# Chunks of one step in a message-passing kernel, and products of constants ahead of two groups of matmuls

## The chip, the cores and the metric

The kernel runs on one core of one Trainium2 chip. The metric is the device time of one execution in microseconds. Before the change the median of three runs is 8919.56 us (8911.16 to 8920.2).

## What is computed

One layer of message passing over a graph of 12500 nodes and 800000 edges, with 64 values per node and 16 per edge. `src` and `dst` are drawn at random, so a node has some 64 edges that come in, in no order.

```python
def reference(x, e_attr, src, dst, w_msg, w_upd):
    N, D = x.shape
    m_in = jnp.concatenate([x[src], x[dst], e_attr], axis=-1)
    msg = _silu(m_in @ w_msg)
    agg = _segment_sum(msg, dst, N)
    return _silu(jnp.concatenate([x, agg], axis=-1) @ w_upd)
```

## The kernel before, in words

**Tiles and buckets.** The edges stand in 6250 tiles of 128. The nodes are split into 128 buckets of 98 nodes (`BK`). Two flows run through one another. The first sorts the edges by the bucket of `dst` into a store in DRAM (`st`). The second reads sorted tiles of the store, works out their messages, and adds them by node into `ACC` on the chip.

**The sort, in steps of 8 tiles (`M`).** A step passes through three calls of `period`: first `onehot` (ACT, L396 and L397) makes `hf`, the one-hot matrix of buckets, and `sums` (L399) adds up to three of its tiles in bfloat16 into `G`. One period later `count` (L418, PE) multiplies these by a triangle and by ones (`onesb`) into `z`, so that `ranks` (L433, DVE) reads the rank of each edge within its bucket and chunk, and `expand` (L435 to L447, DVE) writes the edge's record of 17 numbers (`R`) into the slot of that rank in `X`, which has two buffers. Another period later `move` (L463, PE) multiplies `hf` and `X` into `pl`, in float32: row b of `pl` then holds the records of bucket b. When a chunk ends, ACT copies `pl` to `blk` (L468, two buffers), `place` (L481 and L482, DVE) moves the pointers of the buckets on, and in the next period POOL writes `blk` to the store by one indirect DMA (L486, the scatter).

**Chunks.** The slots of a chunk are shared by its tiles. The first 140 chunks (`N8`) are one step of 8 tiles, with 24 slots at their end. The rest are 12 tiles (`C`), a step and a half, with 30 slots at the end; the limit grows along the chunk (`LIM`: 13, 17, 21, 24, 27, 30, each for two tiles), and the product of a tile is 2 + 17 times its limit columns wide, 223 to 512. A step of this part stands in one of three places against the chunks (`turn` 0, 1, 2). Where a chunk goes on from the step before, the last sum of that step is carried over (`before`, L414, and L409 and L410 through the buffer `Gs`), and `count` adds it by a product of its own (L428). In `turn` 1 a chunk ends in the middle of the step, and `move` is called twice, around the product of the other flow.

**The batches.** A batch is 8 tiles of the store (6 in the second of three stages). POOL gathers a row of 64 values per edge by eight indirect DMAs (L649) into one of four buffers `g`, so the first of them waits for the sums by node of the batch four before. A period later PE transposes the batch's one-hot matrix and edge values (`tq`, L668), ACT copies them (`qt`, L671), and `product` (L677, PE) multiplies them with the weights into `pre`. Then `message` adds `pre` to `g` (L681, DVE) and applies silu (L682, ACT), and a period later `reduce` (L698, PE) sums by node into `ag`, which `add` (L710, DVE) adds to `ACC`.

**The order of the work.** `period` (L715) writes one call's instructions in a fixed order, and each engine takes its own in that order. On POOL that is four gathers, the scatter of a chunk that ended in the period before, four gathers. On PE it is `count`, the transposes, `reduce`, `move`, `product`. There are 782 steps, and 63 batches are left when the last is done. The lines on which the change turns are these:

```python
                for k in reversed(range(c.n)) if whole else range(c.n):
                    n = c.pos[k]
                    if part is not None and part != (c.turn == 1 and k >= C - M):
                        continue
                    ...
                    if ends:
                        w = 2 + LIM[c.size - 1] * R
                        end = Chunk(*c.last.values())
```

Of the kernel before, what the change touches and what calls it, by code (L numbers as in the profile page):

```python
# [3 lines left out]
F32 = mybir.dt.float32  # L4
# [19 lines left out]
C = 12  # L24
N8 = 140
LIM = [k for k in (13, 17, 21, 24, 27, 30) for _ in range(2)]
S = LIM[-1]
S8 = LIM[M - 1]
# [12 lines left out]
RK = float(C * P)  # L41
# [7 lines left out]
def mpnn_kernel(tc, x, e_attr, src, dst, w_msg, w_upd, out):  # L49
# [4 lines left out]
    assert E % P == 0 and NB <= NBK and NT >= C  # L54
    K8 = min(N8, NT // (2 * M))
    NCH = K8 + (NT - K8 * M + C - 1) // C
    CAPT = (K8 * S8 + (NCH - K8) * S) // P + 2
# [15 lines left out]
    with es:  # L73
# [43 lines left out]
        limc = cp.tile([P, 4, M], F32, name="limc")  # L117
        for k in range(4 * M):
            nc.vector.memset(limc[:, k // M, k % M:k % M + 1], RK + LIM[k % M if k >= 3 * M else k % C])

# [6 lines left out]
        Gs = cb[:, P + M * S:2 * P + M * S]  # L127
        ps1 = cb[:, 2 * P + M * S:2 * P + M * S + 1]
# [103 lines left out]

        T1, GAP = NT - (NT - K8 * M) % C, -(NT - K8 * M) % C
        T2 = NT + GAP
        T3 = T2 + -T2 % M

        def spread(buf, src, t0, n):

            clip = lambda t: min(n, max(0, t - t0))
            for a, b, o in ((0, T1, 0), (T1, T1 + GAP, None), (T1 + GAP, T2, GAP), (T2, T3, None)):  # L240
                i, j = clip(a), clip(b)
                if i < j and o is None:
                    nc.vector.memset(buf[:, i:j], 0.0 if buf.dtype == F32 else 0)
                elif i < j:
                    nc.sync.dma_start(buf[:, i:j], src[:, t0 + i - o:t0 + j - o])
# [8 lines left out]
        def seg_prep(di, si, n, t0=0):  # L254
            hi = sg.tile([P, SEG], F32, name="shi")
            lo = sg.tile([P, SEG], F32, name="slo")

            floor_ops(hi[:, :n], lo[:, :n], di[:, :n], -HI_SC, -HI_OFF)
            nc.vector.scalar_tensor_tensor(out=lo[:, :n], in0=hi[:, :n], scalar=float(BK), in1=di[:, :n], op0=OP.mult, op1=OP.add)

            for a, b in ((T1, T1 + GAP), (T2, T3)):
                a, b = max(0, a - t0), min(n, b - t0)
                if a < b:
                    nc.vector.memset(hi[:, a:b], -float(2 * P))
            return hi, lo, si
# [39 lines left out]
        def next_step(ic):  # L305
# [14 lines left out]
            return Step(ready[si][0][:, c0:c0 + M], rec_t[e0][:, eo:eo + M, :], ic - K8, min(M, T2 - ic * M))  # L320
# [56 lines left out]
        prior = dict(step=None, pl=None)  # L377

        class Step:


            def __init__(c, hi, rec, index, n=M):

                c.hi, c.rec, c.n = hi, rec, n
                c.turn = index % 3 if index >= 0 else 3
                c.size = C if index >= 0 else M
                c.pos = [(c.turn * M + k) % C if index >= 0 else k for k in range(M)]
                c.prev, prior["step"] = prior["step"], c

                c.last = {k: K8 + (index * M + k) // c.size for k in range(n) if c.pos[k] == c.size - 1}  # L390
# [8 lines left out]
            def sums(c):  # L399
# [6 lines left out]
                for a in ((0, 1), (1,), (0,), (0,))[c.turn]:  # L406
                    k = c.G[:, a, 2, :]
                    if a == (1 if c.turn == 0 else 0) and c.turn in (0, 2):
                        nc.vector.tensor_tensor(out=Gs, in0=c.before(a), in1=h[:, a, 3, :], op=OP.add)  # L409
                        nc.vector.tensor_tensor(out=c.G[:, a, 3, :], in0=Gs, in1=k, op=OP.add)  # L410
                    else:
                        nc.vector.tensor_tensor(out=c.G[:, a, 3, :], in0=k, in1=h[:, a, 3, :], op=OP.add)

            def before(c, a):  # L414

                return c.G[:, 0, 3, :] if a else c.prev.G[:, 1, 3, :]

            def count(c):  # L418
# [3 lines left out]
                for a in range(2):  # L422
                    k = a * ZB
                    first = c.pos[k] == 0
                    nc.tensor.matmul(c.z[:, k:k + ZB, :], w1, hb[:, k:k + ZB, :], start=True, stop=False)
                    nc.tensor.matmul(c.z[:, k + 1:k + ZB, :], onesb, c.G[:, a, 0:ZB - 1, :], start=False, stop=first)  # L426
                    if not first:
                        nc.tensor.matmul(c.z[:, k:k + ZB, :], onesb, c.before(a)[:, None, :].to_broadcast([P, ZB, NBK]), start=False, stop=True)  # L428
# [6 lines left out]
            def expand(c, rs=None):  # L435
# [6 lines left out]
                nc.vector.tensor_tensor(out=c.x[:, :, 1], in0=rank, in1=limc[:, c.turn, :], op=OP.is_ge)  # L442
                nc.vector.tensor_tensor(out=hit, in0=ioS[:, None, :].to_broadcast([P, M, S]), in1=rank[:, :, None].to_broadcast([P, M, S]), op=OP.is_equal)
                for k in range(0, c.n, 2):
                    n = LIM[c.pos[k]]
# [3 lines left out]
            def move(c, part=None):  # L449

                end = None
                whole = c.turn == 3

                for k in reversed(range(c.n)) if whole else range(c.n):
                    n = c.pos[k]
                    if part is not None and part != (c.turn == 1 and k >= C - M):
                        continue
                    if n == (c.size - 1 if whole else 0):
                        prior["pl"] = pp.tile([P, 512], F32, name="pl")
                    pl = prior["pl"]  # L460
                    w = 2 + LIM[n] * R
                    ends = n == (0 if whole else c.size - 1)
                    nc.tensor.matmul(pl[:, 0:w], c.hf[:, k, :], c.x[:, k, 0:w], start=(n == (c.size - 1 if whole else 0)), stop=ends, skip_group_check=True)  # L463
                    if ends:
                        w = 2 + LIM[c.size - 1] * R
                        end = Chunk(*c.last.values())
                        end.blk = bp.tile([NBK, XR], F32, name="blk")[:, 0:w]
                        nc.scalar.activation(end.blk, pl[:, 0:w], AF.Copy)  # L468
                return end

        class Chunk:


            def __init__(c, index):
                c.index, c.m = index, M if index < K8 else min(C, NT - K8 * M - (index - K8) * C)
# [144 lines left out]
        class Batch:  # L620
# [94 lines left out]
        def period(step=None, batch=None, ptr_new=None):  # L715
# [154 lines left out]
        def step():  # L870
# [5 lines left out]
            if pipe["z"] and pipe["z"].last:  # L876
# [11 lines left out]
            if pipe["z"]:  # L888
                for i in pipe["z"].last.values():
                    draws.place(Chunk(i).m)  # L890
# [176 lines left out]
        with tc.If(more > 0):  # L1067
# [4 lines left out]
            with tc.If(nover > 0):  # L1072
# [23 lines left out]
                rounds = nc.values_load(fi[0:1, 1:2], min_val=0, max_val=C * P // RS + 1, skip_runtime_bounds_check_because="a count of rounds")  # L1096
# [3 lines left out]
                with tc.For_i(0, nover, 1):  # L1100
# [5 lines left out]
                    w0 = cp.tile([1, 4], F32, name="w0")  # L1106

                    nc.vector.tensor_scalar(out=w0[:, 2:3], in0=f1[:, 2:3], scalar1=-float(K8), scalar2=0.0, op0=OP.add, op1=OP.max)
                    nc.vector.tensor_scalar(out=w0[:, 3:4], in0=f1[:, 2:3], scalar1=float(K8), scalar2=float(C - M), op0=OP.is_ge, op1=OP.mult)
                    nc.vector.tensor_scalar(out=w0[:, 2:3], in0=w0[:, 2:3], scalar1=float(C - M), scalar2=None, op0=OP.mult)  # L1110
                    nc.vector.scalar_tensor_tensor(out=w0[:, 2:3], in0=f1[:, 2:3], scalar=float(M), in1=w0[:, 2:3], op0=OP.mult, op1=OP.add)
                    nc.vector.tensor_scalar(out=w0[:, 0:1], in0=w0[:, 2:3], scalar1=float(NT - C), scalar2=None, op0=OP.min)
                    nc.vector.tensor_tensor(out=w0[:, 1:2], in0=w0[:, 2:3], in1=w0[:, 0:1], op=OP.subtract)
                    nc.vector.tensor_scalar(out=w0[:, 2:3], in0=w0[:, 3:4], scalar1=float(M), scalar2=None, op0=OP.add)
                    nc.vector.tensor_copy(fi[:, 2:3], w0[:, 0:1])
                    bps = pp.tile([P, 512], F32, name="bps", tag="pl")
                    nc.tensor.matmul(bps[:, 0:2], oner, w0[:, 1:3], start=True, stop=True)
                    skip = cp.tile([P, 2], F32, name="skip")
                    nc.vector.tensor_copy(skip, bps[:, 0:2])
                    tv = nc.values_load(fi[0:1, 2:3], engines=(ENG.SP,), min_val=0, max_val=NT - C, skip_runtime_bounds_check_because="the start of a chunk")  # L1120
                    window = lambda buf, src: nc.sync.dma_start(buf, src[:, ds(tv, C)])
                    hi, lo, si = seg_prep(*seg_load(window, C), C, -NT)
                    rec = records(ea_load(window, C), si[:, :C], lo[:, :C], C)
                    off = cp.tile([P, C], F32, name="off")
# [62 lines left out]
```

## Time and profile before

| | |
|---|---|
| time, median of 3 runs | 8919.56 us |
| span of the profiled execution | 10886.0 us (its time around the span is not given) |
| mean granted TensorE clock in it | 0.885 |
| gathers (L649), scatters in steps (L486) | 6322 and 567 |
| HBM | 330.05 MB read, 152.30 MB written, 44 GB/s over the span |

The profiled execution is 22% longer than the timed runs. In the rows of a profile, PE is the matmul side of TensorE, PEld its loading of weights, DVE VectorE, ACT ScalarE, POOL GpSimd and SP SyncE. A row of the timeline gives the start and the length in us, the engine, the line, the operation, output <- inputs, how many, and in brackets how long the engine had been idle and what ended that. A row of a group gives the count, the busy us and the mean ns of one, then the idle us before them by what ended it; "issue" is a gap that no wait explains, and "remote" a wait whose releaser was not found. A row by windows gives the stretch, its length, the busy us of PE, PEld, DVE, ACT and POOL with their counts, the granted clock of TensorE, the busy share of the DMA engines, and GB/s.

### The profile page before, as it was taken

The numbers are of one execution on the slowest core, as the hardware profiler recorded it, in microseconds if no ns is written. First come the engines' busy times: TensorE is split into PE (matmuls) and PEld (weight loads), VectorE is DVE, ScalarE is ACT, GpSimd is POOL, SyncE is SP. The second block draws the span as 40 slices with busy tenths as digits, with TensorE's granted clock in tenths as the row PEclk, the third lists the DMA queues.
The fourth block names the chain that finished last, engine by engine and source line by source line (L and its number), as shares of the span: only waits on it lengthen the run. The fifth ranks groups of instructions, "written<-read, shape, count | busy, mean of one in ns | idle before, by whom it ended". The sixth has DMA issues, their size and how long they took to land. (4 is left out here: it accounts for less than half of the span.)

```text
span 10886.0 us, 155616 instructions
## 1 busy us (share of the span) xinstructions
PE 8949.9 (82%) x49053; PEld 6219.2 (57%) x49816; DVE 7231.4 (66%) x15936; ACT 5082.6 (47%) x12594; POOL 6571.4 (60%) x6908
## 2 busy tenths in 40 slices
PE   8788888888888888888888888888888888888556
PEld 5566655555555555555555555555555555555555
DVE  7777776666666666766666666666666666766232
ACT  6455554444444444444444444444444444544211
POOL 2565666666666666666666666666666666666555
PEclk9999998999989988999998999999899998988555
DMA  3111111111111111111111111111111111111212
GB/s 97 44 49 48 49 49 46 43 47 42 47 42 46 45 44 45 44 43 44 46 43 46 44 44 43 46 47 43 45 42 46 43 47 44 44 45 41 46 36 44
DMA packets 662903, 501.15 MB, mean 46 GB/s; under 512 B 492983, under 2 KB 529911, under 8 KB 662071
## 3 DMA queue, kind: packets, MB, share of 16 engines
q0 software_dynamic: 238976, 349.72, 12.3%
q1 hardware_dynamic: 422775, 141.27, 5.9%
q8 instruction: 400, 6.55, 0.3%
q14 instruction: 432, 3.54, 0.1%
q10 hardware_dynamic: 320, 0.07, 0.0%
HBM read 330.05 MB, written 152.30 MB: 44 GB/s over the span
## 5 line engine op out<-in xcount | busy, mean ns | idle before, releaser
L649 POOL DMA_INDIRECT g<-A_d,sidx x6322 | 5997.6, 949 | 3658.7 <-issue 1620.7
L463 PE MATMUL pl<-X,hf 128*128 128x291 f32 (+5 forms) x12512 | 4745.0, 524 | 476.4 <-issue 428.3
L463 PEld LDWEIGHTS pl<-X,hf 128*128 128x128 f32 x12512 | 2538.7, 211 | 2159.4 <-issue 1737.4
L446 DVE TENSOR_TENSOR X<-cb,rec 128x442 f32<-128x442 f32 (+5 forms) x3128 | 2646.6, 908 | 26.7
L396 ACT ACTIVATE hf<-iof,shi 128x128 f32<-128x128 f32 x6256 | 1908.8, 389 | 1360.4 <-PE pl L463 449.0
L671 ACT ACTIVATE qt<-tq 114x1024 f32<-114x1024 f32 (+1 forms) x818 | 811.7, 992 | 2951.3 <-remote 2298.5
L433 DVE TENSOR_REDUCE rank<-z 128x8 f32<-128x1024 f32 x782 | 954.5, 1221 | 1270.3 <-remote 874.9
L677 PEld LDWEIGHTS pre<-w,qt 114*128 114x128 f32 x10496 | 1392.5, 209 | 687.8 <-ACT qt L671 467.1
L677 PE MATMUL pre<-w,qt 114*128 114x64 f32 x10496 | 1395.2, 291 | 345.6 <-ACT qt L671 317.6
L710 DVE TENSOR_TENSOR ACC<-ag,ACC 64x98 f32 x1938 | 496.7, 256 | 1553.3 <-remote 1131.7
L698 PE MATMUL ag<-q,g 128*64 128x98 f32 x12644 | 882.3, 276 | 490.4 <-remote 236.2
L698 PEld LDWEIGHTS ag<-q,g 128*64 128x64 f32 x12644 | 681.6, 151 | 668.8 <-issue 381.7
L668 PE MATMUL tq<-ident,q 128*114 128x128 f32 x6322 | 929.9, 294 | 103.3 <-issue 91.5
L668 PEld LDWEIGHTS tq<-ident,q 128*114 128x114 f32 x6322 | 812.6, 147 | 238.7 <-issue 122.6
L397 ACT ACTIVATE hf<-hf,ones 128x1024 f32<-128x1024 f32 x782 | 898.8, 1149 | 25.4
L486 POOL DMA_INDIRECT st<-blk,ptrs x567 | 567.2, 1000 | 561.4 <-ACT blk L468 272.2
L659 DVE TENSOR_TENSOR q<-cb,lo 128x784 f32<-128x784 f32 (+1 forms) x818 | 768.7, 940 | 96.1 <-PE ag L698 46.3
L468 ACT ACTIVATE blk<-pl 128x512 f32<-128x512 f32 (+1 forms) x568 | 324.9, 572 | 818.2 <-PE pl L463 500.9
L426 PE MATMUL z<-G,onesb 128*128 128x384 bf16 x1564 | 529.8, 339 | 78.9 <-issue 25.2
L682 ACT ACTIVATE g<-g 128x512 f32<-128x512 f32 (+1 forms) x818 | 498.4, 609 | 192.5 <-DVE g L681 111.8
L681 DVE TENSOR_TENSOR g<-pre,g 128x512 f32<-128x512 f32 (+1 forms) x818 | 541.3, 662 | 51.4 <-issue 37.2
L677 PE MATMUL pre<-BW,qt 114*128 (+1 forms) x2148 | 326.3, 314 | 99.0 <-ACT qt L671 64.8
(138 smaller groups left out, 5243.9 us busy)
## 6 DMA issues: line engine op xcount, KB each, us to landing
g<-A_d,sidx POOLq DMA_INDIRECT x6322
ea<-in_e_attr SPq DMA_DIRECT2D x260, 192.0 KB
rt<-st SPq DMA_DIRECT2D x1312, 34.0 KB
st<-blk,ptrs POOLq DMA_INDIRECT x567
rt<-st SPq DMA_DIRECT2D x434, 8.5 KB
nodes<-in_x SPq DMA_DIRECT2D x62, 98.0 KB
ACC<-rt SPq DMA_DIRECT2D x11, 544.0 KB
rt<-st SPq DMA_DIRECT2D x320, 17.0 KB
```

Source lines behind the costliest of these rows:

```text
L396: nc.scalar.activation(c.hf[:, k, :], iof, AF.Square, bias=c.hi[:, k:k + 1])
L397: nc.scalar.activation(c.hf, c.hf, AF.Relu, bias=ones, scale=-1.0)
L433: nc.vector.tensor_reduce(out=c.rank, in_=c.z, axis=AX.X, op=OP.max)
L446: nc.vector.tensor_tensor(out=c.x[:, k:k + 2, 2:2 + n * R].rearrange("p k (s c) -> p k s c", c=R), in0=hit[:, k:k + 2, 0:n, None].to_broad ...
L463: nc.tensor.matmul(pl[:, 0:w], c.hf[:, k, :], c.x[:, k, 0:w], start=(n == (c.size - 1 if whole else 0)), stop=ends, skip_group_check=True)
L486: i = nc.gpsimd.indirect_dma_start(out=st, out_offset=bass.IndirectOffsetOnAxis(ap=c.ptr, axis=0), in_=c.blk[:, 2:], in_offset=None)
L649: j = nc.gpsimd.indirect_dma_start(out=t.g[:, i, :], out_offset=None, in_=A_d, in_offset=bass.IndirectOffsetOnAxis(ap=t.grp.sidx[:, k:k + ...
L659: nc.vector.tensor_tensor(out=t.q[:, 0:n, 0:BK], in0=ioB[:, None, :].to_broadcast([P, n, BK]), in1=t.grp.lo[:, i0:i0 + n, None].to_broadca ...
L668: nc.tensor.transpose(t.tq[0:KQ, j * P:(j + 1) * P], t.q[:, j, :], ident)
L671: nc.scalar.activation(t.qt[:, 0:w], t.tq[0:KQ, 0:w], AF.Copy)
L677: nc.tensor.matmul(t.pre[:, i * D:(i + 1) * D], t.qt[:, i * P:(i + 1) * P], w, start=True, stop=True)
L698: o = nc.tensor.matmul(t.ag[t.half(v), v // 2 * BK:(v // 2 + 1) * BK], t.g[:, i, :], t.q[:, i, 0:BK], start=(k == 0), stop=(k == u - 1))
```

## The change

A chunk is now always one step of 8 tiles. `LIM` is 13, 17, 21, 25, each for two tiles, so a chunk ends with 25 slots, and the product of a tile is 223 to 427 columns wide. There are 782 chunks for 568. `C`, `N8`, the turns, the carried sum and its buffer `Gs`, and the tiles that stood empty where two sizes met all go; `move` is one call, before `product`, from the last tile of the step to the first, and each period ends with a copy of `pl` to `blk` and a `place`. The part of the program that repeats a chunk whose slots overflowed is rewritten for this. A new function `fill` issues three bfloat16 products of `onesb` with itself, 512 columns each, into a PSUM bank that the next products overwrite; it is called ahead of `product` and ahead of `reduce`.

```diff
-C = 12
-N8 = 140
-LIM = [k for k in (13, 17, 21, 24, 27, 30) for _ in range(2)]
+LIM = [k for k in (13, 17, 21, 25) for _ in range(2)]
...
-    NCH = K8 + (NT - K8 * M + C - 1) // C
+    NCH = (NT + M - 1) // M
...
-                for a in ((0, 1), (1,), (0,), (0,))[c.turn]:
-                    k = c.G[:, a, 2, :]
...
+                nc.vector.tensor_tensor(out=c.G[:, 0, ZB - 1, :], in0=c.G[:, 0, ZB - 2, :], in1=h[:, 0, ZB - 1, :], op=OP.add)
...
-                    if not first:
-                        nc.tensor.matmul(c.z[:, k:k + ZB, :], onesb, c.before(a)[:, None, :].to_broadcast([P, ZB, NBK]), start=False, stop=True)
+                nc.tensor.matmul(c.z[:, ZB:M, :], onesb, c.G[:, 0, ZB - 1, None, :].to_broadcast([P, ZB, NBK]), start=False, stop=True)
...
+            def move(c):
+
+                pl = pp.tile([P, 512], F32, name="pl")
+                for k in reversed(range(c.n)):
+                    w = 2 + LIM[k] * R
+                    nc.tensor.matmul(pl[:, 0:w], c.hf[:, k, :], c.x[:, k, 0:w], start=(k == c.n - 1), stop=(k == 0), skip_group_check=True)
+                end = Chunk(c.index)
+                w = 2 + LIM[c.n - 1] * R
+                end.blk = bp.tile([NBK, XR], F32, name="blk")
...
+                nc.scalar.activation(end.blk[:, 0:w], pl[:, 0:w], AF.Copy)
                 return end
...
+            def fill(t, ps):
+                for _ in range(3):
+                    nc.tensor.matmul(ps[:, 0:4 * P].rearrange("p (a b) -> p a b", b=P), onesb, onesb[:, None, :].to_broadcast([P, 4, P]), start=True, stop=True)
+
             def product(t):
                 t.pre = ppre.tile([P, 512], F32, name="pre")
+                t.fill(t.pre)
...
             def reduce(t):
                 t.ag = pag.tile([P, 512], F32, name="ag")
+                t.fill(t.ag)
...
             if p:
-                e = p.move(0)
+                e = p.move()
             if t:
                 t.product()
-            if p:
-                p.move(1)
```

On PE, one period in the middle of the program before the change, from the transposes of a batch on; the step is in `turn` 1, so its last four tiles (L463, X to `pl`) end one chunk and its first four begin another:

```order
L668 MATMUL tq<-ident,q 114x128 x8
L698 MATMUL ag<-q,g_222 64x98 x8
L463 MATMUL pl<-X_184,hf 128x461 x2
L463 MATMUL pl<-X_184,hf 128x512 x2
L677 MATMUL pre<-w,qt 128x64 x8
L463 MATMUL pl<-X_184,hf 128x223 x2
L463 MATMUL pl<-X_184,hf 128x291 x2
```

And one period after it; L635 is `fill`, L628, L664, L422 and L642 are what L668, L698, L463 and L677 were, and each of the two fills stands there three times in all:

```order
L628 MATMUL tq<-ident,q 114x128 x8
L635 LDWEIGHTS onesb
L635 MATMUL ag<-onesb 128x512
L664 MATMUL ag<-q,g_193 64x98 x8
L422 MATMUL pl<-X_155,hf 128x427 x2
L422 MATMUL pl<-X_155,hf 128x359 x2
L422 MATMUL pl<-X_155,hf 128x291 x2
L422 MATMUL pl<-X_155,hf 128x223 x2
L635 LDWEIGHTS onesb
L635 MATMUL pre<-onesb 128x512
L642 MATMUL pre<-w,qt 128x64 x8
```

The four tiles that stood behind the product now stand ahead of it, none is wider than 427 columns, and six bfloat16 products are new. On POOL, three batches before the change (L649 gathers into the buffers `g`, L486 scatters `blk`):

```order
L486 DMA st<-blk,ptrs 2938112x17
L649 DMA g_221<-A_d,sidx 128x64 x4
L649 DMA g_222<-A_d,sidx 128x64 x4
L486 DMA st<-blk,ptrs 2938112x17
L649 DMA g_222<-A_d,sidx 128x64 x4
L649 DMA g_223<-A_d,sidx 128x64 x8
L649 DMA g_220<-A_d,sidx 128x64 x4
L486 DMA st<-blk,ptrs 2938112x17
```

And after it, where L609 gathers and L446 scatters:

```order
L446 DMA st<-blk,ptrs 3364096x17
L609 DMA g_192<-A_d,sidx 128x64 x4
L609 DMA g_193<-A_d,sidx 128x64 x4
L446 DMA st<-blk,ptrs 3364096x17
L609 DMA g_193<-A_d,sidx 128x64 x4
L609 DMA g_194<-A_d,sidx 128x64 x4
L446 DMA st<-blk,ptrs 3364096x17
```

Before, two batches of three had a scatter among their gathers; now every batch has one. The number of gathers and their order against the steps are the same.

More of the change, by code (lines that the diff above doesn't have):

```diff
@@ L115, in mpnn_kernel @@
         nc.vector.tensor_scalar(out=b98, in0=ipf, scalar1=float(BK), scalar2=None, op0=OP.mult)
[L117 to L119 removed]
+        limc = cp.tile([P, M], F32, name="limc")
+        for k in range(0, M, 2):
+            nc.vector.memset(limc[:, k:k + 2], RK + LIM[k])
         cb = pc.tile([P, 512], F32, name="cb")
@@ L375, in mpnn_kernel @@
         live = []
-        prior = dict(step=None, pl=None)
         class Step:
             def __init__(c, hi, rec, index, n=M):
[L384 to L390, printed above, removed]
+                c.hi, c.rec, c.index, c.n = hi, rec, index, n
             def onehot(c):
@@ L446, in expand @@
                     nc.vector.tensor_tensor(out=c.x[:, k:k + 2, 2:2 + n * R].rearrange("p k (s c) -> p k s c", c=R), in0=hit[:, k:k + 2, 0:n, None].to_broadcast([P, 2, n, R]),
                                             in1=c.rec[:, k:k + 2, None, :].to_broadcast([P, 2, n, R]), op=OP.mult)
[L449 to L468, printed above, removed]
@@ L875, in step @@
             pn = None
-            if pipe["z"] and pipe["z"].last:
+            if pipe["z"]:
                 if flow["npl"] % 64 == 0:
@@ L888, in step @@
             if pipe["z"]:
-                for i in pipe["z"].last.values():
-                    draws.place(Chunk(i).m)
+                draws.place(Chunk(pipe["z"].index).m)
             period(c, b, pn)
@@ L1119, in mpnn_kernel @@
[L1119 to L1124, printed above, removed]
@@ new lines, in mpnn_kernel @@
+                    skip = cp.tile([P, 1], F32, name="skip")
+                    nc.vector.tensor_copy(skip, bps[:, 0:1])
+                    tv = nc.values_load(fi[0:1, 2:3], engines=(ENG.SP,), min_val=0, max_val=NT - M, skip_runtime_bounds_check_because="the start of a chunk")
+                    window = lambda buf, src: nc.sync.dma_start(buf, src[:, ds(tv, M)])
+                    hi, lo, si = seg_prep(*seg_load(window, M), M)
+                    rec = records(ea_load(window, M), si[:, :M], lo[:, :M], M)
@@ new lines, in mpnn_kernel @@
+                    off = cp.tile([P, M], F32, name="off")
+                    nc.vector.tensor_scalar(out=off, in0=iof[:, 0:M], scalar1=skip, scalar2=float(2 * P), op0=OP.is_lt, op1=OP.mult)
+                    nc.vector.tensor_tensor(out=hi[:, :M], in0=hi[:, :M], in1=off, op=OP.subtract)
+                    c = Step(hi[:, 0:M], rec[:, 0:M, :], 0)
+                    c.onehot()
+                    c.sums()
+                    c.count()
+                    c.ranks()
+                    def block(rs=None):
+                        c.expand(rs)
+                        return c.move()
```

94 lines of the change are left out of this document (29 added, 65 removed).

## The prediction

> **What bounds the kernel now.** I read the page first, then the groups by line, then the timeline of POOL alone, then that of all engines, then the windows by stage.
>
> ```profile
> span 10886.0 us, 155616 instructions
> PE 8949.9 (82%) x49053; PEld 6219.2 (57%) x49816; DVE 7231.4 (66%) x15936; ACT 5082.6 (47%) x12594; POOL 6571.4 (60%) x6908
> ```
>
> By busy shares PE is the bound and POOL has 40% to spare. But this execution took 10886 us where the timed runs took 8919.56, so it is 1966 us (22%) slower than what is to be predicted, and something in it does not exist in the timed runs. The groups show what POOL's idle time is made of:
>
> ```profile
> L649 POOL DMA_INDIRECT g<-A_d,sidx x6322 | 5997.6, 949 | 3658.7 <-issue 1620.7 <-remote 1272.5 <-PE ag L698 387.9
> L463 PE MATMUL pl<-X,hf 128*128 128x291 f32 (+5 forms) x12512 | 4745.0, 524 | 476.4 <-issue 428.3
> L428 PE MATMUL z<-G,onesb 128*128 128x512 bf16 x996 | 393.3, 395 | 1.1 <-DVE X L446 1.1
> L468 ACT ACTIVATE blk<-pl 128x512 f32<-128x512 f32 (+1 forms) x568 | 324.9, 572 | 818.2 <-PE pl L463 500.9
> L486 POOL DMA_INDIRECT st<-blk,ptrs x567 | 567.2, 1000 | 561.4 <-ACT blk L468 272.2 <-issue 161.2 <-ACT nodes L196 99.4
> ```
>
> The timeline of POOL in the middle of the program shows both kinds of gap. A batch is eight gathers, here with one scatter among them:
>
> ```profile
> 5010.81 0.95 POOL L649 DMA_INDIRECT g<-A_d,sidx  x1 [2.44 <-remote]
> 5012.06 0.94 POOL L649 DMA_INDIRECT g<-A_d,sidx  x1 [0.30 <-issue]
> 5013.30 0.95 POOL L649 DMA_INDIRECT g<-A_d,sidx  x1 [0.31 <-issue]
> 5014.56 0.95 POOL L649 DMA_INDIRECT g<-A_d,sidx  x1 [0.30 <-DMA g<-A_d,sidx]
> 5015.81 1.00 POOL L486 DMA_INDIRECT st<-blk,ptrs  x1 [0.31 <-issue]
> 5017.11 0.96 POOL L649 DMA_INDIRECT g<-A_d,sidx  x1 [0.30 <-issue]
> ...
> 5020.88 0.94 POOL L649 DMA_INDIRECT g<-A_d,sidx  x1 [0.30 <-issue]
> 5024.34 0.95 POOL L649 DMA_INDIRECT g<-A_d,sidx  x1 [2.52 <-DVE g L681]
> ```
>
> Inside a batch the gathers start 1.25 us apart (5010.81 to 5012.06) and the scatter takes 1.30 (5015.81 to 5017.11), whatever else runs. Only the first gather of a batch waits, some 2.4 us more or less every time. That gather is the one with a wait on PE (the sums by node of four batches before, L698). In this execution PE's signals come late:
>
> ```profile
> 4003.48 1.25 PE L698 MATMUL ag<-q,g 128*64 128x98 f32 x16
> 4005.97 0.53 DVE L710 TENSOR_TENSOR ACC<-ag,ACC 64x98 f32 x2 [1.43 <-PE ag L698]
> 4006.20 0.94 POOL L649 DMA_INDIRECT g<-A_d,sidx  x1 [2.38 <-PE ag L698]
> ...
> 4011.74 0.20 PE L587 MATMUL ps<-mat,b 128*1 128x16 f32 x2
> 4018.32 0.17 DVE L592 SCALAR_TENSOR_TENSOR row<-ps,iof 1x16 int32<-1x16 f32 x1 [4.24 <-remote]
> ```
>
> The sums end at 4004.73; DVE and POOL, which both wait for them, start at 5.97 and 6.20. The product of L587 ends at 4011.94 and its reader, idle, starts 6.4 us later. I take these delays to be the profiler's, since the timed runs have no room for them, as this sum shows. POOL's own row, with no wait: 6322 gathers by 1.25 us and 567 scatters by 1.30 make 7902 + 737 = **8640 us**. Around it lie the start and the end:
>
> ```profile
> 200.12 0.97 POOL L649 DMA_INDIRECT g<-A_d,sidx  x1 [13.37 <-DVE sidx L530]
> 10848.35 0.94 POOL L649 DMA_INDIRECT g<-A_d,sidx  x1 [0.30 <-issue]
> ...
> 200.00:420.00 220.00, 155.70 (x800) 103.87 (x812) 151.89 (x399) 96.37 (x231) 114.72 (x119) 0.87 0.17 42
> 420.00:1500.00 1080.00, 899.64 (x5043) 658.18 (x5139) 829.64 (x2177) 565.30 (x1391) 652.25 (x680) 0.92 0.20 49
> 1500.00:10040.00 8540.00, 7200.67 (x39375) 4890.93 (x40016) 5864.87 (x12378) 4117.20 (x10269) 5298.65 (x5565) 0.91 0.17 45
> 10040.00:10886.00 846.00, 520.01 (x3136) 453.13 (x3134) 228.60 (x595) 156.38 (x313) 482.41 (x511) 0.58 0.23 42
> ```
>
> 200 us pass before the first gather and 37 after the last one has started. From 200 to 420 us there are 119 POOL instructions, 149 us at 1.25, in 220: 71 us are lost to a thin supply of groups. The scatters alone, by the same stages:
>
> ```profile
> 0.00:200.00 200.00, 21.91 (x22) 0.97 0.45 116
> 420.00:1500.00 1080.00, 97.05 (x97) 0.92 0.20 49
> 1500.00:10040.00 8540.00, 429.45 (x429) 0.91 0.17 45
> ```
>
> 22 of them lie in the first 200 us, 29 us that the sum would count twice. 8640 + 200 + 37 + 71 - 29 is 8919, where the runs took 8919.56; so close a meeting is partly luck, since the start need not take 200 us in a timed run. Still, I read the timed kernel as bound by POOL's issue of indirect transfers, and the profiled one as that row stretched by waits for PE.
>
> **The change, part by part.** *Scatters.* Each chunk is one scatter. Before, 140 chunks have 8 tiles and 428 have 12; after, all 782 have 8: 214 more, all after step 140, that is in the main stage (1500 to 10040 us of the profile). Each takes a slot of 1.30 us between gathers: **+278 us**. It can be no less than 0, if POOL had waits to fill in the timed runs, and the sum above leaves it none. A scatter carries fewer bytes (25 slots for 30); its 1.00 us is the same in the stage before 1500 us, where most have 24 slots, and in the one after, where they have 30 (97.05 over 97, 429.45 over 429), so I count nothing for that.
> By durations instead of spacing the 214 would cost 214 x 1.00 = 214 us. The Trainium skill (Perfetto Trace Analysis, GPSIMD Engine Instruction) says to time GpSimd by start-to-start spacing, not by the span that is shown; the 0.30 us between any two rows here agrees, and only the spacing adds up to the measured time.
>
> *The products into slots (L463).* A chunk of 12 has 223 to 512 columns, mean 376; a chunk of 8 now has 223, 291, 359, 427, mean 325. Two bursts of one step price a column:
>
> ```profile
> 4004.66 3.53 PE L463 MATMUL pl<-X,hf 128*128 128x461 f32 x8
> 4009.76 1.95 PE L463 MATMUL pl<-X,hf 128*128 128x223 f32 x8
> 4008.02 1.90 PE L677 MATMUL pre<-w,qt 114*128 114x64 f32 x16
> ...
> 4012.27 0.39 PE L425 MATMUL z<-hf,w 128*128 128x512 bf16 x1
> 4012.50 0.32 PE L426 MATMUL z<-G,onesb 128*128 128x384 bf16 x1
> 4012.66 0.38 PE L428 MATMUL z<-G,onesb 128*128 128x512 bf16 x1
> 4012.87 1.03 PE L668 MATMUL tq<-ident,q 128*114 128x128 f32 x8
> ```
>
> The first is four tiles of 461 and 512 columns, the second four of 223 and 291, two passes each: 229.5 columns x 8 passes apart, 1.58 us, 0.86 ns a column. A step saves 51 x 16 x 0.86 = 0.70 us of PE, over 642 steps 450 us. The carry of the count (L428) goes from 996 to 783 products, 213 x 0.21 = 45 us.
>
> *The fills.* Three 512-column bfloat16 products ahead of the sums and three ahead of the product, six in a batch. The trace has none, but L428 is the same form with the same weights: from its start to the next it holds PE 0.21 us (4012.66 to 4012.87), L425 0.23. Six take 1.3 us, or twice that at half clock, and over 818 batches 1060 us. They wait for nothing that the next product doesn't wait for already (the bank's last reader, by DVE), so they add length and no new wait.
>
> *Does PE now exceed POOL?* A step of before, by the bursts above (their ends overlap, so this is high): 3.53 + 1.95 + 1.90 + 1.25 + 1.03 and 1.0 for the count, 10.7 us. After: 10.7 - 0.70 - 0.07 + 1.3 = **11.2**, against POOL's 8 x 1.25 + 1.30 = **11.30**, up from a mean of 10.87. PE stays under POOL, narrowly by this high sum. In the stage with batches of six (106 of them, about 420 to 1500 us) POOL needs 8.8 us and PE 6/8 of its batch work, 4.47 + 1.0 + 3.1 + 1.3 = 9.9; there the fills can show, 0 to 1.1 us a batch, 0 to 117 us; I take half, **+55**.
>
> *The rest.* DVE and ACT: narrower expansions and no carried sums on DVE, but 214 more placements, and 214 more evictions of 0.57 us on ACT, which is 47% busy. Under POOL's 11.3 us this costs nothing; without that cover ACT's evictions would be 122 us. Scatters now follow each step, and `blk` has two buffers, so an eviction waits for the scatter of two steps before, some 22 us earlier: no stall while POOL issues steadily. In the last stage (POOL alone, no steps) the fills lie beside eight gathers a batch.
>
> Sum: 8919.6 + 278 + 55 = **9253 us**. The sum is made on POOL's row without waits, which is the timed runs' own time; against the profile's span of 10886 the same terms hold as additions, except that there PE's late signals are the bound and the fills would show as well.
>
> **The rivals.** *PE-bound.* If POOL's spacing is shorter without the profiler, PE is the bound, and the change costs it 1060 - 450 - 45 = +565 us: 9485. For it: PE's 82% and its high sum of 10.7 against 10.87. Against it: POOL's sum meets the measured time.
>
> *Faster: the fills cost nothing and the narrow products count.* PE idles in the profile before L463 alone for 476 us; where PE waits anyway, fills run in those waits, and they keep its clock up. The clock is 0.91 in the main stage, so 18% of it ran at half speed; a full clock would be worth up to 0.09 x 8540 = 769 us there. Then 450 + 45 us are saved: 8425, or anything up to 8919. It decides only if POOL's spacing in the timed runs falls under about 1.2 us a transfer, since 6322 + 781 of them at 1.25 can't fit in less than 9190 with start and end. The Trainium skill (TensorE: Matmul & The Clock Gate, HAM oscillation) has the rule behind this: a gap of more than about 3.4 us returns the clock to half, and PE should be kept without such gaps. The trace agrees on the half clock; whether timed runs have such gaps no run here shows.
>
> *No change.* The scatters fall into waits that POOL has in the timed runs too, and the fills into PE's: 8920.
>
> **How the numbers follow.** POOL-bound 0.70 (9170 to 9330, by the stage of six and a tenth of the scatters hidden); PE-bound 0.15 (9330 to 9500); faster 0.10 (8425 to 8900); no change 0.05. Slower 0.85, same 0.05, faster 0.10, where 0.2% is about what a measurement of this kernel can tell. The predicted time is the likeliest case's, 9250; the range takes in that case with more of the scatters hidden, and PE's: 9110 to 9500.
>
> **What would show it.** In the profile after: 6322 gathers still 1.25 us apart and about 781 scatters 1.30 apart; six products of onesb a batch at 0.21 us; the mean of L463 lower. The profiled span may grow by more than the timed run, as PE's signals are late there. It would be wrong if gathers stand closer than 1.25 us, if the time after is under 9100, or if leaving the fills out of the changed kernel gives back much more than the 55 us that I put on them (then PE is the bound); putting back chunks of 12 without fills should give back the 278.

## The result

The kernel after takes **9300.28 us** (four runs, 9299.06 to 9303.5) beside 8918.99 us for the kernel before: a ratio of 1.0428, 95% interval [1.0414, 1.0443], 381 us more. The prediction was 9250 us, 9110 to 9500. The kernel before took 8911 to 8920 us in these runs and in the first set of experiments, but 10871 to 10928 us in two further sets on two other chips, much as in its first profile (10886), so each experiment is compared with the kernel before of its own set.

A second profile of the kernel before, taken in the first set, lasted 8909.5 us. It is the one to hold against the profile after (9297.3 us). The page of before, second profile:

```profile
span 8909.5 us, 155616 instructions
PE 8172.1 (92%) x49053; PEld 5891.9 (66%) x49816; DVE 7251.2 (81%) x15936; ACT 5059.8 (57%) x12594; POOL 6585.5 (74%) x6908
```

And of after:

```profile
span 9297.3 us, 164827 instructions
PE 8603.6 (93%) x53734; PEld 6172.1 (66%) x54498; DVE 6910.1 (74%) x15692; ACT 5092.1 (55%) x12808; POOL 6804.0 (73%) x7122
```

By shares PE is the busiest in both, and POOL seems to have a quarter to spare. The groups of POOL say otherwise. Before, second profile:

```profile
L649 POOL DMA_INDIRECT g<-A_d,sidx x6322 | 6012.1, 951 | 1948.9 <-issue 1521.4 <-DMA g<-A_d,sidx 254.5 <-PE ag L698 37.2
L486 POOL DMA_INDIRECT st<-blk,ptrs x567 | 566.8, 1000 | 315.0 <-issue 156.4 <-ACT nodes L196 99.4 <-ACT blk L468 38.4
```

After:

```profile
L609 POOL DMA_INDIRECT g<-A_d,sidx x6322 | 6015.0, 951 | 2037.1 <-issue 1532.7 <-DMA g<-A_d,sidx 221.0 <-PE ag L664 133.7
L446 POOL DMA_INDIRECT st<-blk,ptrs x781 | 782.4, 1002 | 396.3 <-issue 195.2 <-ACT nodes L191 97.1 <-ACT blk L428 54.0
```

Add the busy time and the idle time ahead of it. The gathers take 7961.0 us before and 8052.1 after, 91.1 more; the scatters 881.8 and 1178.7, 296.9 more. Together that is 388.0 us, and the spans differ by 387.8. That the two agree proves nothing yet, since an engine's busy and idle time together fill the span whether it is the bound or not. What tells is the idle time ahead of one row. POOL in the main stage alone (1500 to 8800 us), after:

```profile
L609 POOL DMA_INDIRECT g<-A_d,sidx x5147 | 4897.0, 951 | 1568.8 <-issue 1225.0 <-DMA g<-A_d,sidx 207.3 <-DVE ptrs L442 53.3
L446 POOL DMA_INDIRECT st<-blk,ptrs x630 | 631.3, 1002 | 192.0 <-issue 184.7 <-ACT g L647 2.4 <-ACT G L383 2.4
```

On the mean that is 0.30 us ahead of each gather and of each scatter, the gap that stands between any two rows of POOL here (before, second profile, 1500 to 8400 us: 1542.6 us over 5062 gathers, 0.30 too). So in the main stage POOL works without a wait in both kernels, and the scatters' part of the difference is mostly their number (214 more, 1.30 us each, are 278). The gathers' part is a wait: 133.7 us for PE's sums over the whole run where it was 37.2.

POOL in the middle of the program, after:

```profile
5001.55 1.00 POOL L446 DMA_INDIRECT st<-blk,ptrs  x1 [0.30 <-issue]
5002.85 0.96 POOL L609 DMA_INDIRECT g<-A_d,sidx  x1 [0.30 <-issue]
5004.12 0.94 POOL L609 DMA_INDIRECT g<-A_d,sidx  x1 [0.30 <-issue]
...
5011.60 0.95 POOL L609 DMA_INDIRECT g<-A_d,sidx  x1 [0.30 <-issue]
5012.86 1.00 POOL L446 DMA_INDIRECT st<-blk,ptrs  x1 [0.31 <-issue]
```

From scatter to scatter it is 11.31 us, with eight gathers between and never more than 0.31 us from one row to the next. In the stage with batches of six it is different. After:

```profile
700.12 0.95 POOL L609 DMA_INDIRECT g<-A_d,sidx  x1 [0.96 <-PE ag L664]
701.37 0.96 POOL L609 DMA_INDIRECT g<-A_d,sidx  x1 [0.30 <-issue]
...
705.26 1.00 POOL L446 DMA_INDIRECT st<-blk,ptrs  x1 [0.44 <-ACT blk L428]
...
709.74 0.94 POOL L609 DMA_INDIRECT g<-A_d,sidx  x1 [0.96 <-PE ag L664]
```

A batch takes 9.62 us (700.12 to 709.74) where POOL's own seven slots are 8.80: the first gather waits 0.66 us beyond the usual 0.30, the scatter 0.14. By this one batch, 106 of them lose some 87 us.

### The profile page after: what moved, and what is told of

It is laid out like the page before. It is cut to its first block, busy times and chain, and to the rows that moved or that the text cites. A ratio compares the mean times of both kernels' runs of the same rounds, so it can differ in the third digit from the quotient of the medians.

```text
span 9297.3 us, 164827 instructions
## 1 busy us (share of the span) xinstructions
PE 8603.6 (93%) x53734; PEld 6172.1 (66%) x54498; DVE 6910.1 (74%) x15692; ACT 5092.1 (55%) x12808; POOL 6804.0 (73%) x7122
## 5 line engine op out<-in xcount | busy, mean ns | idle before, releaser
L609 POOL DMA_INDIRECT g<-A_d,sidx x6322 | 6015.0, 951 | 2037.1 <-issue 1532.7
L422 PE MATMUL pl<-X,hf 128*128 128x427 f32 (+3 forms) x12500 | 3629.3, 442 | 99.8 <-ACT blk L428 97.4
L422 PEld LDWEIGHTS pl<-X,hf 128*128 128x128 f32 x12500 | 2302.8, 189 | 1268.5 <-issue 530.3
L414 DVE TENSOR_TENSOR X<-cb,rec 128x442 f32<-128x442 f32 (+3 forms) x3125 | 2376.0, 822 | 26.8
L428 ACT ACTIVATE blk<-pl 128x427 f32<-128x427 f32 x782 | 412.1, 527 | 3483.5 <-DMA st<-blk,ptrs 1978.8
L642 PEld LDWEIGHTS pre<-w,qt 114*128 114x128 f32 x10496 | 1288.7, 194 | 97.9 <-ACT qt L631 3.3
L642 PE MATMUL pre<-w,qt 114*128 114x64 f32 x10496 | 1257.2, 273 | 0.1
L446 POOL DMA_INDIRECT st<-blk,ptrs x781 | 782.4, 1002 | 396.3 <-issue 195.2
L628 PE MATMUL tq<-ident,q 128*114 128x128 f32 x6322 | 911.4, 291 | 15.0 <-ACT nodes L191 13.7
L628 PEld LDWEIGHTS tq<-ident,q 128*114 128x114 f32 x6322 | 804.3, 145 | 144.5 <-issue 25.4
L635 PE MATMUL pre<-onesb 128*128 128x512 bf16 x2454 | 680.6, 387 | 188.7 <-DVE g L646 182.8
L635 PEld LDWEIGHTS <-onesb 128*128 128x128 bf16 x4908 | 470.1, 101 | 567.8 <-DVE g L646 176.4
L664 PEld LDWEIGHTS ag<-q,g 128*64 128x64 f32 x12644 | 589.4, 139 | 375.8 <-issue 315.5
L664 PE MATMUL ag<-q,g 128*64 128x98 f32 x12644 | 747.5, 257 | 0.0
L635 PE MATMUL ag<-onesb 128*128 128x512 bf16 x2454 | 715.1, 403 | 13.7 <-DVE rb L553 12.1
```

The source lines that it names most:

```text
L414: nc.vector.tensor_tensor(out=c.x[:, k:k + 2, 2:2 + n * R].rearrange("p k (s c) -> p k s c", c=R), in0=hit[:, k:k + 2, 0:n, None].to_broad ...
L446: i = nc.gpsimd.indirect_dma_start(out=st, out_offset=bass.IndirectOffsetOnAxis(ap=c.ptr, axis=0), in_=c.blk[:, 2:], in_offset=None)
L609: j = nc.gpsimd.indirect_dma_start(out=t.g[:, i, :], out_offset=None, in_=A_d, in_offset=bass.IndirectOffsetOnAxis(ap=t.grp.sidx[:, k:k + ...
L628: nc.tensor.transpose(t.tq[0:KQ, j * P:(j + 1) * P], t.q[:, j, :], ident)
L635: nc.tensor.matmul(ps[:, 0:4 * P].rearrange("p (a b) -> p a b", b=P), onesb, onesb[:, None, :].to_broadcast([P, 4, P]), start=True, stop=True)
L642: nc.tensor.matmul(t.pre[:, i * D:(i + 1) * D], t.qt[:, i * P:(i + 1) * P], w, start=True, stop=True)
```

## The experiments

**First set: where the time went.** The theory is that POOL's issue sets the time and the fills cost only in the stage of six. The rival is that PE is the bound, so that the fills are most of the cost and the narrower products give some of it back. The kernel before took 8915.83 us in this set.

*The kernel before again, no edit, for its profile.*

> The kernel before, unchanged, for a second profile. Theory (POOL's issue bounds the timed kernel, and late signals of PE stretch the profiled one): the timed execution stays at 8919 us and the profiled span is again far above it, 10400 to 11000, with some 2.4 us ahead of the first gather of a batch. Rival (the first profile was one odd execution): a span of about 8920, gathers 1.25 us apart through the main stage, no wait ahead of a batch.

It took 8911.32 us, and its span is the 8909.5 us above. POOL at the same place as in the prediction's timeline:

```profile
5007.69 0.94 POOL L649 DMA_INDIRECT g<-A_d,sidx  x1 [0.30 <-DMA g<-A_d,sidx]
5008.94 1.00 POOL L486 DMA_INDIRECT st<-blk,ptrs  x1 [0.30 <-issue]
5010.25 0.96 POOL L649 DMA_INDIRECT g<-A_d,sidx  x1 [0.30 <-issue]
5011.51 0.94 POOL L649 DMA_INDIRECT g<-A_d,sidx  x1 [0.30 <-issue]
```

There is no 2.4 us wait ahead of the first gather of a batch: the rival of this run held, and not the theory. A profile can be free of these waits, so profiling alone does not make them.

*The changed kernel without fills.*

```diff
-                t.fill(t.pre)
...
-                t.fill(t.ag)
```

> The changed kernel without its two calls of fill; the output is the same. Theory (POOL bounds all but the stage with batches of six, where PE's 9.6 us a period stand against POOL's 8.8): 9300 less 0.82 x 106 = 87 us, 9190 to 9225 us. Rival, PE bounds throughout: six products of 0.21 us in each of 818 batches come back, 1060 us, 8240 to 8500. Second rival, the fills keep PE's clock up: slower than 9300, with a clock like that of the profile of before (0.89).

Measured: 9203.44 us, ratio 1.0321 [1.0304, 1.0339]. The chunks alone cost 288 us, the fills 97. The rows of POOL, PE and ACT in this kernel:

```profile
L609 POOL DMA_INDIRECT g<-A_d,sidx x6322 | 6019.7, 952 | 1948.0 <-issue 1489.0 <-DMA g<-A_d,sidx 266.9 <-DVE ptrs L442 78.9
L446 POOL DMA_INDIRECT st<-blk,ptrs x781 | 782.2, 1002 | 384.6 <-issue 220.3 <-ACT nodes L191 98.3 <-DVE X L414 24.3
L422 PE MATMUL pl<-X,hf 128*128 128x427 f32 (+3 forms) x12500 | 3659.3, 445 | 575.8 <-ACT blk L428 565.6 <-DVE LOST L441 8.9 <-DVE X L414 0.3
L428 ACT ACTIVATE blk<-pl 128x427 f32<-128x427 f32 x782 | 412.0, 527 | 3397.9 <-DMA st<-blk,ptrs 2831.7 <-PE pl L422 372.2 <-PE ag L662 130.0
```

The second profile of before has for the same product:

```profile
L463 PE MATMUL pl<-X,hf 128*128 128x291 f32 (+5 forms) x12512 | 4201.9, 487 | 4.8 <-DVE LOST L481 4.1 <-ACT blk L468 0.6
```

The narrower products saved PE 543 us (4201.9 to 3659.3) and in their place PE waits 566 us for ACT to empty `pl`. ACT waits 2832 us for the scatter that frees `blk`, and POOL issues that scatter in its turn. The saving went into a queue behind POOL. POOL's own sum is 7967.7 us for the gathers, 6.7 more than before, and 1166.8 for the scatters, 285.0 more.

*The changed kernel with fills left out only where batches have six gathers.*

```diff
-                for _ in range(3):
+                for _ in range(0 if t.grp.bt == 6 else 3):
```

> The changed kernel with fills in all batches but those of six tiles. Theory: the fills cost only in the stage of six, so this is the same as leaving all of them out, 9190 to 9225 us, within 20 us of that kernel. Rival, the fills cost in the main stage too: 712 of 818 batches still pay, 9150 to 9300 here and the kernel with no fills several hundred us faster than this one.

Measured: 9203.11 us, 1.0321 [1.0304, 1.0339], the same as with no fills at all. The fills of the main stage cost nothing and those of the stage of six cost all of the 97 us. The windows of that stage (busy us of PE, PEld, DVE, ACT, POOL with their counts) for this kernel:

```profile
420.00:1500.00 1080.00, 1028.71 (x6359) 760.34 (x6474) 986.16 (x2548) 687.03 (x1717) 821.27 (x850) 1.00 0.26 62
```

and for after, with the main stage under it:

```profile
420.00:1500.00 1080.00, 1061.53 (x6394) 752.13 (x6501) 927.01 (x2402) 633.17 (x1582) 743.71 (x776) 1.00 0.25 57
1500.00:8000.00 6500.00, 6090.03 (x38400) 4360.09 (x38974) 4943.92 (x10828) 3688.26 (x9356) 4929.95 (x5152) 0.98 0.24 56
```

With the fills POOL gets 776 transfers into these 1080 us, without them 850; 74 at 1.27 us are 94 us. PE is busy for 98% of the stage and 94% of the main one.

*The kernel before with the fills.*

```diff
+            def fill(t, ps):
+                for _ in range(3):
+                    nc.tensor.matmul(ps[:, 0:4 * P].rearrange("p (a b) -> p a b", b=P), onesb, onesb[:, None, :].to_broadcast([P, 4, P]), start=True, stop=True)
...
+                t.fill(t.pre)
...
+                t.fill(t.ag)
```

> The kernel before with the same fills ahead of product and reduce. Theory: 87 us in the stage of six, and in the main stage PE's step (9.7 us by starts, and 1.3 for the fills) comes to 11.0 against POOL's mean of 10.87, so 0.1 to 0.5 us a step over 642 steps: 9050 to 9330. Rival, PE bounds before too: 1060 us more, 9900 to 10000. Second rival, the fills help by the clock: under 8919.

Measured: 9144.4 us, 1.0256 [1.0239, 1.0273], 229 us more. So on chunks of 12 the fills cost 229 and on chunks of 8 only 97. Its windows, and those of the kernel before, second profile:

```profile
420.00:1500.00 1080.00, 1059.55 (x6365) 748.00 (x6473) 934.16 (x2394) 628.98 (x1570) 742.62 (x777) 1.00 0.24 56
1500.00:8000.00 6500.00, 6454.91 (x39332) 4389.37 (x39915) 5365.38 (x11248) 3732.43 (x9345) 4847.66 (x5064) 1.00 0.23 53
```

```profile
420.00:1500.00 1080.00, 1025.99 (x6306) 757.93 (x6421) 1006.48 (x2565) 690.09 (x1724) 821.27 (x850) 1.00 0.26 60
1500.00:8000.00 6500.00, 6086.09 (x36541) 4303.36 (x37135) 5470.92 (x11478) 3805.76 (x9530) 4925.68 (x5167) 0.96 0.23 54
```

The stage of six loses 73 transfers, as the changed kernel lost 74. In the main stage PE is now busy for 99% (6454.91 of 6500), and POOL issues 103 transfers fewer. Its scatters now wait for `blk`, which ACT fills from PE's `pl` (220.7 us where the second profile of before has 38.4):

```profile
L486 POOL DMA_INDIRECT st<-blk,ptrs x567 | 567.2, 1000 | 434.6 <-ACT blk L468 220.7 <-ACT nodes L196 100.3 <-issue 86.2
```

PE has become the bound there by a little. The rival of a bound by PE is right for this kernel, and wrong for the changed one, whose products are 51 columns narrower a tile.

**Second and third set: what a slot on POOL is worth.** The two sets ran on two other chips, where the kernel before took 10900.67 and 10904.22 us. The expectations were written for 8916 us, and what they say of the kernel before holds there only as a difference.

*A ninth gather ahead of each batch of the main loop, into a buffer that nobody reads: on the kernel before, and on the kernel after.*

```diff
+        spare = lp.tile([P, D], F32, name="spare")
...
+                if lo and state["straight"]:
+                    nc.gpsimd.indirect_dma_start(out=spare, out_offset=None, in_=A_d, in_offset=bass.IndirectOffsetOnAxis(ap=t.grp.sidx[:, t.i0:t.i0 + 1], axis=0))
```

> The kernel before with a ninth indirect gather in each batch, into a tile that nobody reads; the output is the same. Theory, POOL's issue bounds the kernel before from its first batch to its last: 818 more transfers at 1.25 us, 1022 us, 8916 + 1022 = 9938 us (9900 to 9960). Rival, PE bounds before, close above POOL: the added transfers fill POOL's waits first, and the time grows by clearly less, 9000 to 9800.

> The kernel before with one more gather ahead of each batch that the main loop issues (818 batches), whose rows nobody reads. In the first set of runs its time stood beside a kernel before of 10900 us, so the price of a POOL slot could only be read there (+1065 us). POOL-bound: where the kernel before takes 8916 us, 818 x 1.25 = 1022 us more, 9940 (9850 to 10050). Rival, PE is the bound and POOL has some 20% to spare: no more than 8920 to 9100.

> The changed kernel with the same ninth gather. Theory: the main and the last stage pay 1.25 us a batch (712 batches, 890 us), the stage of six only what goes beyond PE's 9.6 us a period (8.8 + 1.25 - 9.6 = 0.43 us, 106 batches, 46 us): 9300 + 936 = 10236 us (10200 to 10270). Rival, POOL bounds the stage of six too and the fills cost their 97 us elsewhere: 9300 + 1022 = 10322.

On the kernel before: 11966.13 us, 1.0978 [1.0957, 1.0999], in the second set and 11992.48 us, 1.0999 [1.0979, 1.1018], in the third: 1065 and 1088 us more, for 818 slots, 1.30 and 1.33 us each. The expectations named 9938 and 9940 us, from a kernel before of 8916; as a difference they named 1022, and both sets lie a little above it: 1065 is over the range of the second set (984 to 1044), 1088 within the wider one of the third. On the kernel after: 12441.86 us, 1.1416 [1.1397, 1.1435], which is 476 us above the kernel before with a ninth gather. The expectations have 298 there (10236 less 9938), so this one missed; the changed kernel without a ninth gather was not run on this chip, and what the slot costs it stays open. POOL's timeline of the kernel before with the ninth gather, third set:

```profile
5002.94 0.94 POOL L650 DMA_INDIRECT g<-A_d,sidx  x1 [2.72 <-remote]
5004.19 0.94 POOL L650 DMA_INDIRECT g<-A_d,sidx  x1 [0.30 <-issue]
...
5014.26 0.94 POOL L657 DMA_INDIRECT spare<-A_d,sidx  x1 [0.30 <-issue]
5017.97 0.94 POOL L650 DMA_INDIRECT g<-A_d,sidx  x1 [2.77 <-remote]
```

The batch has one slot more, and the wait ahead of it is still there, 2.7 us. A wait of 2 us or more ahead of each batch took up none of a 1.25 us slot. So a slot added on POOL is paid for in full even where POOL waits; what the wait hangs on in these runs is not shown, and a ninth gather was not run on the chip where the kernel before takes 8916 us.

*The changed kernel without fills and with wider products: limits of 17, 21, 25, 25, a mean of 376 columns as in the kernel before.*

```diff
-LIM = [k for k in (13, 17, 21, 25) for _ in range(2)]
+LIM = [k for k in (17, 21, 25, 25) for _ in range(2)]
...
-                t.fill(t.pre)
...
-                t.fill(t.ag)
```

> The changed kernel without fills and with limits of 17, 21, 25 and 25 slots, whose mean of 22 (376 columns) is that of the kernel before: it gives back the 450 us of PE that the narrower products saved, and keeps the 214 further scatters. POOL-bound: the narrower products were hidden, so nothing shows: 9203 (9195 to 9240). Rival, the narrower products are on the path and made up for part of what else the change costs: 9203 + 450 = 9650, or 9300 and more in any case.

Measured: 11162.97 us, 1.0235 [1.0218, 1.0252], 259 us more than the kernel before of its set (238 to 275), and not the 9203 that was expected from a kernel before of 8916. It is 1.11 to 1.28 us for each of the 214 scatters, at equal widths and without fills. Its rows on POOL:

```profile
L609 POOL DMA_INDIRECT g<-A_d,sidx x6322 | 5982.7, 946 | 3641.3 <-issue 1613.9 <-remote 1032.1 <-PE ag L662 398.4
L446 POOL DMA_INDIRECT st<-blk,ptrs x781 | 779.8, 998 | 659.1 <-ACT blk L428 303.6 <-issue 204.0 <-ACT nodes L191 112.8
```

Against the first profile of before, which stands in the prediction, the gathers' row gives 32 us back (9656.3 to 9624.0) and the scatters' row takes 310 (1128.6 to 1438.9). That the narrower products gain nothing where the kernel before takes 8916 us rests on the run without fills, not on this one: this chip is another, and the narrow kernel without fills was not run on it.

*Six fills for each three.*

```diff
-                for _ in range(3):
+                for _ in range(6):
```

> The changed kernel with six products in each fill for three. Theory: PE's step in the main stage, 10.2 us by starts with the fills as they are, comes to 11.5 against POOL's 11.3 and becomes the bound there, 0.2 to 0.5 us a step over 642 steps, and the stage of six pays the whole 1.29 x 106 = 137 us: 9560 to 9800. Rival, PE has more room than that and only the stage of six pays: 9430 to 9450.

> The changed kernel with six fills for each three, so twelve a batch. POOL-bound with PE just beneath it: the fills of the changed kernel showed only where batches have six gathers; six more a batch are 6 x 0.215 = 1.29 us, and PE stands at POOL's 11.3 us a batch or just under it, so the most of them shows now: 9300 + 818 x 1.29 = 10355 at most, and 9300 + 106 x 1.29 = 9437 at least if PE still has 1.3 us to spare in the main stage. From the kernel before with fills, whose products are 0.6 us a step wider and where PE stood 0.2 us a step above POOL, PE here has some 0.5 us to spare in the main stage: 0.8 us x 690 + 1.29 x 106 = 690 us more, 9990 (9700 to 10150). Rival, fills raise PE's clock and cost little: under 9440.

Measured: 11634.91 us, 1.0684 [1.0664, 1.0705], and 11647.23 us, 1.068 [1.0662, 1.0697]. The changed kernel itself was not run on these chips, so what the second three cost can't be told. Inconclusive: how much room PE has left in the main stage of the changed kernel stays open.

*The kernel before with 60 chunks of 8 tiles in place of 140, which has 27 scatters fewer: a try at a faster version.*

```diff
-N8 = 140
+N8 = 60
```

> The kernel before with 60 chunks of 8 tiles ahead of those of 12, for 140: 27 scatters fewer, and 80 steps of wider products in the stage of six. Theory: 27 x 1.30 = 35 us less if POOL stays the bound there, 8880 us; PE's step of about 9.1 us there (with the wider products, no fills) against POOL's 7.5 + 0.87 = 8.4 gives back up to 0.7 x 80 = 56 us, so 8875 to 8940. Rival, the larger chunks starve the groups of tiles early on: over 8950.

> The kernel before with N8 = 60 in place of 140: 80 steps of 8 tiles fewer have a chunk of their own, so 27 scatters fewer. POOL-bound: 27 x 1.30 = 35 us less, 8881 (8870 to 8905), if the groups still fill as early. Rivals: the groups fill later and POOL waits for them early on, 8920 to 8960; scatters cost nothing, 8916.

Measured: 10904.5 us, 1.0004 [0.9993, 1.0015], and 10919.58 us, 1.0012 [0.9999, 1.0025]. The 35 us did not appear. POOL's rows in the third set:

```profile
L649 POOL DMA_INDIRECT g<-A_d,sidx x6322 | 5988.9, 947 | 3714.8 <-issue 1627.0 <-remote 1341.9 <-PE ag L698 423.6
L486 POOL DMA_INDIRECT st<-blk,ptrs x540 | 539.4, 999 | 554.9 <-ACT blk L468 281.7 <-issue 138.2 <-ACT nodes L196 105.8
```

Against the first profile of before the scatters' row falls by 34 us (1128.6 to 1094.3), as expected, and the gathers' row grows by 47 (9656.3 to 9703.7), in its waits. But the edit does two things: it also puts wider products into 80 steps of the stage of six, which the expectation of the second set priced at up to 56 us. From 420 to 1500 us PE is busy for 952.46 us in this run and for 899.64 in the first profile of before, and POOL issues 589 gathers for 583, though it has 25 scatters fewer there (72 for 97). So the run does not show whether a slot taken away is given back, here or where the kernel before takes 8916 us.

## Why the prediction was right, and where it was not

**POOL's row as the bound: right, though the sum met its mark by luck.** The second profile shows POOL without waits in the main stage, as the profile of after does; the fills of the main stage cost nothing, and the chunks cost 1.34 us for each further scatter, about one slot of POOL. But "8640 + 200 + 37 + 71 - 29" was made of terms that were off against one another. The 200 us before the first gather are there in the short profile too (200.3). The end after the last gather is 20 us and not 37, and the thin supply from 200 to 420 us, where it has 152 transfers in place of 119, costs some 29 us and not 71. With these values the sum is 8860, 49 us under the span of 8909.5. The transfers stand a little further apart than the sum has them: by 1.25 and 1.30 us, 4769 gathers and 398 scatters would need 6479 of the 6500 us from 1500 to 8000, and 741 and 109 would need 1068 of the 1080 in the stage of six, 33 us in these two alone.

**"I take these delays to be the profiler's": wrong.** A profile of the same kernel has none of them and lasts 8909.5 us, and on two other chips the medians of 13 runs each were 10901 and 10904 us. (Of the 6.4 us between the product of L587 and its reader, the reader's own row has it idle for 4.24.) The conclusion drawn from it, that a time of 8919 leaves no room for the waits, held all the same.

**The scatters, +278: right.** The chunk part measured 288 us at the narrow widths, 1.34 us a scatter. By durations it would have been 214, which is outside the interval of 271 to 302. The Trainium skill (Perfetto Trace Analysis, GPSIMD Engine Instruction), which says to take start-to-start spacing, agrees here. On the other chip the price was 1.11 to 1.28, between spacing and duration.

**The narrower products, -450 on PE, and the carries, hidden: right.** Without fills the products' busy time fell by 543 us, more than the 450, and came back as 566 us of waiting for ACT. The step on `blk` ("no stall while POOL issues steadily") needs mending: there is a stall, 2832 us on ACT, only it lies behind POOL and costs nothing.

**The fills, +55: the right place and the wrong size.** They cost 97 us, inside the bounds of 0 to 117, and all of it in the stage of six. Half of the upper bound was taken, which is a choice and not a price. The short profile of before, which came only after the prediction, has PE busy for 1025.99 of 1080 us in that stage, 8.36 us of each 8.80; with six products by 0.21 that is 9.62, as in the batch shown above. So close a meeting is luck: from 420 to 1200 us the profile of after has 79 batches, 9.9 us each. The first profile gave 9.9 by adding bursts, a value that the prediction had and did not take. (The prediction's working is not even: it has the same four pairs of products at 4.47 us in this stage and at 3.53 + 1.95 - 0.70 = 4.78 in the main one.) This term is 42 of the 47 us by which the sum of 9253 fell short; the chunks, at 288 for 278, are 10 more, and the kernel before, 4 us faster in the first set, takes 4 off.

**The rivals.** *PE-bound, 9485*: no, but close by: on chunks of 12 the same fills make PE the bound of the main stage. The two parts of the change don't add: 288 and 229 us apart would be some 517, together they cost 381, since the narrower products make room for the fills. *Faster, by a better clock*: the fills did raise the granted clock, from 0.941 (changed kernel without them) to 0.962, and on the kernel before from 0.939 to 0.983, and the time rose by 97 and 229 us. The clock had little to give where PE is the bound: in the stage of six it stands at 1.00 before, without any fill, and in the main stage of before at 0.96, where POOL is the bound. The rule that the prediction cited for this rival (the Trainium skill, TensorE: Matmul & The Clock Gate, HAM oscillation) has PE kept without long gaps. The runs agree in that the fills went with a higher clock; the length of gap that it names no run here shows. *No change*: no; even on chips where POOL waits ahead of each batch, the scatters cost 259 us.

## What to carry to other kernels

Where one engine issues transfers at a fixed spacing, divide the idle time ahead of its rows by their number, stage by stage: if what is left is only the gap that stands between any two of them, the engine is the bound, though it shows 74% busy, and each transfer costs its spacing. Price an edit on another engine by that engine's share of the stage, not of the span, for a stage with less work per batch is where it shows. And look at a profile's span against the timed runs before reading its waits: if they differ, look for a profile that agrees, and don't decide by argument what made the difference.

## What the runs showed of the hardware

The kernel before took 8915.83 us on one chip and 10900.67 and 10904.22 us on two others, 22% longer; on which chip its first profile, also a long one, was taken is not on record. In the long runs PE's own waits are of another kind. Ahead of the product into slots it idles 428.3 us by "issue" in the first profile of before, and 640.9 in the kernel with the ninth gather,

```profile
L464 PE MATMUL pl<-X,hf 128*128 128x291 f32 (+5 forms) x12512 | 4913.4, 535 | 690.4 <-issue 640.9 <-ACT blk L469 13.4 <-DVE X L447 8.0
```

where the short profile of before has 4.8 us of idle time in all at that line. The granted clock is lower with it (0.885 for the first profile, 0.85 for the ninth gather, 0.939 for the short profile), while the gathers' own length hardly differs (949, 948 and 951 ns). No run here shows what makes these chips or these times different.
